# A windowed-attention and gated feed-forward kernel: sign words on GpSimd, one shift-and-sign instruction, and one eviction in two halves

## The chip, the cores and the metric

The kernel runs on one core of a Trainium2 chip. The metric is device time in microseconds (us) of one launch, as the median over several runs; lower is better. The core's engines are TensorE (PE in the profile, with PEld for its weight loads), VectorE (DVE), ScalarE (ACT), GpSimd (POOL) and SyncE (SP, which here only issues DMAs). Every engine works through its own queue in order, and engines wait for one another through semaphores.

## The reference

Eight heads of attention over 576 positions, batch 8, head dimension 64; heads 0 to 3 see the last 32 positions, heads 4 to 7 see every fourth of the last 128. Then a feed-forward layer on the 4608 tokens with 512 inputs and 2048 hidden units:

```python
scores = (q @ k.T) / 8, outside the mask -1e9
attn   = softmax(scores)
x      = (attn @ v) laid out as [4608, 512]
h      = x @ w_in                       # [512, 2048]
g      = h * clip(h + 3, 0, 6) / 6
out    = g @ w_out                      # [2048, 512], float32
```

`w_in` and `w_out` arrive as 64-bit floats. The kernel gets them as 64-bit words, and has to turn them into 32-bit floats itself.

## The kernel before

**Attention.** The 64 pairs of batch and head are worked in 48 "trios" of three 128-row parts (384 columns); each is a block of small 64-row matmuls for scores (L245), a largest value and an exponent, a transpose through TensorE (L374), a block of small matmuls for values (L255), a normalisation (L330 to L333), another transpose, and a split of the result into a high and a low part (L473, L479). The first twelve trios stand in the first stage.

**Weights.** There are 32 weight pieces of 128 by 512 elements: piece 2f is slab f of `w_in`, piece 2f+1 slab f of `w_out`. A piece p is loaded (`w`, L510) into a tile `st` of 64-bit words, that is, of a high and a low 32-bit word in turn, and then passes through these named steps:

- `Q` (`cv_round`, ACT, L529): the top bits of the low words, into `a`.
- `U` (`cv_product`, ACT, L525): the high words, read as 32-bit floats, times 2 to the power -112, into `v`.
- `s` (`cv_shift`, DVE, L533): `v` shifted left by three, in place.
- `j` (`cv_sign`, DVE, L539): the sign bit of the high words put into `v`, in place.
- `a` (`cv_add`, DVE, L546): `v` plus `a`, as integers.
- `h` (`cv_high`, ACT, L549) and `l` (`cv_low`, DVE, L555): the high part and the rest, which are what TensorE multiplies with.

**Feed-forward.** `G` (L571 to L573, twelve matmuls into one of two `ps_h` banks), `RE` (ACT, L579), `T` (DVE, L582, reads the bank and so frees it), `GH` (ACT or GpSimd, L586), `GL` (DVE, L590) and `H` (L632, nine matmuls). High and low parts make three products out of each one. The first `G` and `H` run while weights are still being turned; the later token groups run another scheme of seven products each (L784, L793 to L795), whose operands are sums of the weights.

**Order.** The first stage (to about 160 us) follows an order written out by hand, the string `ORDER` (L58 to L80): its names are issued in this order on ACT, DVE, SP and TensorE. `s4 CX4 j4` is step `s` of piece 4, a copy, and step `j` of piece 4. A name `w2@a0` is a load that SP holds back until `a0` is done; among the loads held back in this way are `k5@R3` (`R` is the largest value of a trio, L282), `v3@j0` and `v6@j2`. `Dn` stands for 2n fill matmuls on TensorE (L186). After the first stage a planner (`_in_time`) orders all engines from estimated durations. GpSimd has no order by hand in the first stage; its instructions are placed there by the framework's own scheduler, and there were none between the start and the planner's part.

**End.** In the last token group the last product (`T4`) is computed for its last two weight pairs one output half after the other (`parts` (0,) and then (1,)), each half one PSUM bank of 128 by 512. `scaled` (L1143) copies a bank to SBUF times one sixth on ACT (L1150), and `ship` (L1186) writes it out (L1190).

Of the kernel before, what the change touches and what calls it, by code (L numbers as in the profile page):

```python
# [13 lines left out]
U32 = mybir.dt.uint32  # L14
I64 = mybir.dt.int64
AF = mybir.ActivationFunctionType
ALU = mybir.AluOpType
# [7 lines left out]
CG = 512  # L25
# [61 lines left out]
def windowed_attention_ffn(ctx: ExitStack, tc: tile.TileContext, qk, vp, w, mask, out, out_t):  # L87
# [23 lines left out]
    nc = tc.nc  # L111
# [49 lines left out]
    def mask_of(kind, part, rows=P):  # L161
# [6 lines left out]
        out=ident, in_=ident, compare_op=ALU.not_equal, fill=1.0, base=0, pattern=[[-1, P]], channel_multiplier=1  # L168
# [32 lines left out]
    def w_tile(name, shape, dtype=F32):  # L201
        return wpool.tile([P, *shape], dtype, name=name, tag="w")
# [314 lines left out]
    def parts(p):  # L517
        st, va = staged[p]
        words = st.rearrange("p a n -> p (a n)").rearrange("p (n w) -> p n w", w=2)
        return words[:, :, 1], words[:, :, 0], va[:, 0], va[:, 1]  # L520
# [7 lines left out]
        _, lo_w, _, a = parts(p)  # L528
        return nc.scalar.mul(a.bitcast(U32), lo_w.bitcast(U32), 2.0**-29)  # L529

    def cv_shift(p):
        v = parts(p)[2]
        return nc.vector.tensor_scalar(  # L533
            out=v.bitcast(U32), in0=v.bitcast(U32), scalar1=3, scalar2=None, op0=ALU.logical_shift_left
        )

    def cv_sign(p):
        hi_w, _, v, _ = parts(p)
        return nc.vector.scalar_tensor_tensor(  # L539
            out=v.bitcast(U32), in0=hi_w.bitcast(U32), scalar=0x80000000, in1=v.bitcast(U32),  # L540
            op0=ALU.bitwise_and, op1=ALU.bitwise_or,
        )

    def cv_add(p):
# [256 lines left out]
    def load_mask(i):  # L801
# [13 lines left out]
        "Y": turn_x, "CX": turned_x,  # L815
        "XH": high, "XL": lambda t: low(t, nc.vector),

        "U": cv_product, "Q": cv_round, "s": cv_shift, "j": cv_sign, "a": cv_add, "h": cv_high, "l": cv_low,

        "G": gemm1, "RE": relu, "T": gate, "GH": gate_high, "GL": gate_low, "H": gemm2,  # L820
    }
# [3 lines left out]
    def op(engine, us, do, after=(), lag=0.0, takes=(), gives=(), before=(), ahead=AHEAD):  # L825
        plan.append(Operation(engine, us, do, [x for x in after if x is not None], lag, [(*x, 0)[:3] for x in takes], list(gives), list(before), ahead))
        if engine == "PE":
            beats.append(len(plan) - 1)
        return len(plan) - 1
# [309 lines left out]
    def second_products(g):  # L1139

        banks, lows, sums_of, os, made, read_by = {}, {}, {}, {}, {}, {}

        def scaled(name, bank, x, frees=False, parts=range(2)):  # L1143

            ops = []
            for d in parts:
                def do(d=d):
                    if name not in os:
                        os[name] = w_tile("o", [2, CG])
                    nc.scalar.mul(os[name][:, d], banks[bank][d], 1.0 / 6.0)  # L1150

                y = op("ACT", 0.6, do, [x], takes=() if d else SLOT, gives=FREE if frees else ())
                if frees:
                    freed.append(y)
                ops.append(y)
            made[name] = ops
            return ops
# [98 lines left out]
        def ends(p, x, parts):  # L1256

            if p == R11:
                read_by["x"] = read_by["y"] = seed(x)
            elif p == R21:  # L1260
                ship("11", scaled("11", "y", x, True))
            elif p == T1:
                read_by["w"] = scaled("22", "w", x)
            elif p == T2:
                read_by["x"] = scaled("12", "x", x)
            elif p == R22:
                ship("12", added("12", "w", x, True))
            elif p == T3:
                read_by["x"] = added("22", "x", x)
                ship("22", read_by["x"])  # L1270
            else:
                last_parts.extend(scaled("21", "x", x, True, parts))
                if len(parts) == 1:
                    ship("21", last_parts, slice(parts[0], parts[0] + 1))
                elif parts[-1] == 1:
                    ship("21", last_parts)
# [26 lines left out]
    with tc.manual_schedule(  # L1303
# [3 lines left out]
        for name in ORDER.split():  # L1307
            name, _, behind = name.partition("@")
# [261 lines left out]
```

## Time and profile before

| what | value |
|---|---|
| median of 3 runs | 825.68 us (823.89 to 826.71) |
| the profiled execution, its own time | 829.52 us |
| its span, first to last instruction | 827.7 us |
| TensorE busy | 814.9 us, 98% of the span |
| VectorE busy | 639.5 us, 77% |
| ScalarE busy | 512.4 us, 62% |
| GpSimd busy | 122.5 us, 15% |
| mean granted TensorE clock | 0.995 |

The page divides the span into 40 slices of 20.7 us. A row of a group gives the line, engine, operation, what it writes and reads, the shape and the count, then the busy time and the mean duration of one in ns, and the idle time of that engine before it with what ended it. A row of a timeline gives start and duration in us, engine, line and operation. A row of windows gives for each stretch its length and the busy time of every engine.

### The profile page before, as it was taken

What the parts mean: (1) busy time and instruction counts of PE and PEld (TensorE: products, weight loads), DVE (VectorE), ACT (ScalarE), POOL (GpSimd) and SP (SyncE); (2) the same over time, 40 slices, a digit from 0 to 9 for tenths busy, and PEclk for the clock granted to TensorE, in tenths of its full rate; (3) what the DMA queues carried; (4) which work ended last, traced back from release to release, by engine and by line L of the source; (5) the groups of instructions that cost most, each with busy time, mean ns of one, the idle gap of its engine ahead of it and who ended that gap; (6) DMA issues with size and microseconds to landing.
All of it is one profiled execution on the core that took longest, in us unless ns stands there. A gap on an engine that the chain in (4) does not pass through costs nothing.

```text
span 827.7 us, 20447 instructions
## 1 busy us (share of the span) xinstructions
PE 814.9 (98%) x8095; PEld 687.5 (83%) x8095; DVE 639.5 (77%) x1189; ACT 512.4 (62%) x1148; POOL 122.5 (15%) x268
## 2 busy tenths in 40 slices
PE   8799999999999999999999999999999999999998
PEld 5589989899888889878888888888888888888886
DVE  4699999568787998998989996575798934459943
ACT  3488776346877875677877565585565524446542
POOL 0000000013554454112360001031000000000000
PEclk9899999999999999999999999999999999999999
DMA  7847433336767879999985656786539369560632
GB/s 238 279 158 228 149 127 103 117 131 198 255 197 233 287 256 349 363 314 391 394 321 178 229 178 225 277 293 232 178 103 314 124 232 389 211 225 30 216 140 77
DMA packets 99343, 184.92 MB, mean 223 GB/s; under 512 B 6448, under 2 KB 35120, under 8 KB 99248
## 3 DMA queue, kind: packets, MB, share of 16 engines
q1 hardware_dynamic: 99248, 183.62, 64.4%
q8 instruction: 64, 1.05, 0.5%
q14 instruction: 31, 0.25, 0.1%
HBM read 144.79 MB, written 38.80 MB: 222 GB/s over the span
## 4 chain that ended last, share of the span: by engine, by line
PE 96%; ACT 2%; DVE 1%; issue 1%
PE ps_o L784 28%; PE ps_o L632 15%; PE ps_x L793 9%; PE ps_x L794 9%; PE ps_x L795 9%; PE ps_h L571 5%; PE ps_h L572 5%; PE ps_h L573 5%; PE ps_a L263 2%; PE ps_a L245 2%; PE ps_a L255 1%; PE ps_b L263 1%; PE ps_b L245 1%; PE ps_a L374 1%; PE idle L186 1%
## 5 line engine op out<-in xcount | busy, mean ns | idle before, releaser
L784 PE MATMUL ps_o<-gh,ring 128*128 128x512 f32 x672 | 182.5, 390 | 0.0
L784 PEld LDWEIGHTS ps_o<-gh,ring 128*128 128x128 f32 x672 | 126.2, 188 | 26.1
L1230 DVE TENSOR_TENSOR gl<-g,gh 128x512 fp32r<-128x512 f32 x168 | 109.1, 688 | 23.6 <-ACT gh L1226 17.8
L1226 ACT CAST gh<-g 128x512 fp32r<-128x512 f32 x168 | 97.0, 622 | 37.7 <-PE ps_o L784 36.8
L784 PE MATMUL ps_o<-gl,ring 128*128 128x512 f32 x336 | 103.8, 390 | 0.0
L632 PE MATMUL ps_o<-wo,gh 128*128 128x512 f32 x372 | 95.5, 392 | 0.0
L793 PE MATMUL ps_x<-cells,ring 128*128 128x512 f32 x240 | 94.1, 392 | 0.0
L795 PE MATMUL ps_x<-cells,ring 128*128 128x512 f32 x240 | 93.5, 390 | 0.0
L571 PE MATMUL ps_h<-x,wi 128*128 128x384 f32 x256 | 87.6, 342 | 0.0
L572 PE MATMUL ps_h<-x,wi 128*128 128x384 f32 x256 | 86.2, 337 | 0.0
L573 PE MATMUL ps_h<-x,wi 128*128 128x384 f32 x256 | 86.2, 337 | 0.0
L632 PEld LDWEIGHTS ps_o<-wo,gh 128*128 128x128 f32 x372 | 68.7, 188 | 11.5 <-DVE o L926 0.5
L784 PEld LDWEIGHTS ps_o<-gl,ring 128*128 128x128 f32 x336 | 63.1, 188 | 13.0
L794 PE MATMUL ps_x<-cells,ring 128*128 128x512 f32 x176 | 68.6, 390 | 0.0
L579 ACT ACTIVATE t<-ps_h,three 128x384 f32<-128x384 f32 x64 | 37.0, 581 | 41.0 <-PE ps_h L573 37.2
L794 PE MATMUL ps_x<-cell,ring 128*128 128x512 f32 x160 | 62.4, 390 | 0.0
L1198 DVE TENSOR_TENSOR g<-g 128x1024 f32<-128x1024 f32 x48 | 58.0, 1222 | 0.1
L586 POOL CAST gh<-t 128x384 fp32r<-128x384 f32 x36 | 24.4, 679 | 214.8 <-DVE t L582 200.0
L1095 DVE TENSOR_TENSOR g<-ps_x,g 128x512 f32<-128x512 f32 x48 | 33.1, 689 | 28.8 <-ACT g L1088 25.9
L1088 ACT COPY g<-ps_x 128x512 f32<-128x512 f32 x48 | 28.1, 586 | 42.6 <-PE ps_x L795 40.4
L793 PEld LDWEIGHTS ps_x<-cells,ring 128*128 128x128 f32 x240 | 45.1, 188 | 9.3
L795 PEld LDWEIGHTS ps_x<-cells,ring 128*128 128x128 f32 x240 | 45.1, 188 | 9.4
(137 smaller groups left out, 1665.3 us busy)
## 6 DMA issues: line engine op xcount, KB each, us to landing
ring<-sums SPq DMA_DIRECT2D x84, 512.0 KB, 8.6
ring<-rights SPq DMA_DIRECT2D x84, 512.0 KB, 4.8
st<-in_w SPq DMA_DIRECT2D x32, 512.0 KB, 4.4
kq<-in_qk SPq DMA_DIRECT2D x39, 416.0 KB, 4.6
v<-in_v SPq DMA_DIRECT2D x39, 390.0 KB, 5.8
sums<-wi SPq DMA_DIRECT2D x24, 256.0 KB, 6.8
rights<-wo SPq DMA_DIRECT2D x24, 256.0 KB, 6.1
out<-o SPq DMA_DIRECT2D x11, 512.0 KB, 3.3
```

The costliest lines, as they stand in the source:

```text
L571: nc.tensor.matmul(ph, lhsT=wt(f, 0)[:, ks], rhs=a, start=(kt == 0), stop=False)
L572: nc.tensor.matmul(ph, lhsT=wt(f, 0)[:, ks], rhs=b, start=False, stop=False)
L573: ins = nc.tensor.matmul(ph, lhsT=wt(f, 1)[:, ks], rhs=a, start=False, stop=(kt == NK - 1))
L579: return nc.scalar.activation(ts[n], phs[n], AF.Relu, bias=three, scale=1.0)
L632: ins = nc.tensor.matmul(po[c][tt], lhsT=g[:, tt * P : (tt + 1) * P], rhs=wt(f, row), start=(f == 0 and not i), stop=(f == NF - 1 and i == 2))
L784: nc.tensor.matmul(banks[part], lhsT=right[:, a, cols], rhs=x, start=(start and not i), stop=(i == 2), skip_group_check=True)
L793: nc.tensor.matmul(bank, lhsT=tile_[:, 0, ks], rhs=h[:, kt], start=(start and kt == 0), stop=False, skip_group_check=True)
L794: nc.tensor.matmul(bank, lhsT=tile_[:, 0, ks], rhs=l[:, kt], start=False, stop=False, skip_group_check=True)
L795: nc.tensor.matmul(bank, lhsT=tile_[:, 1, ks], rhs=h[:, kt], start=False, stop=(kt == 1), skip_group_check=True)
L1198: nc.vector.tensor_tensor(out=at[0], in0=at[1], in1=at[2], op=alu)
L1226: nc.scalar.copy(two[0], gated_tile(g, q, k))
L1230: nc.vector.tensor_tensor(out=two[1], in0=gated_tile(g, q, k), in1=two[0].bitcast(F32), op=ALU.subtract)
```

## The change

`s` becomes an instruction of GpSimd: it reads the high words as floats and writes, in their place in `st`, 2 to the power 31 as an integer where the float is negative, and 0 elsewhere. `j` becomes one VectorE instruction that shifts `v` left by three and puts the sign word in. The names keep their places in `ORDER`, and `a`, `h` and `l` are untouched. The last eviction of the kernel becomes two instructions of 128 by 256, the left half on ACT and the right half on DVE, with the same output DMA behind both.

```diff
+    def cv_sign(p):
+        hi_w = parts(p)[0]
+        return nc.gpsimd.tensor_scalar(
+            out=hi_w.bitcast(U32), in0=hi_w, scalar1=0.0, scalar2=2.0**31, op0=ALU.is_lt, op1=ALU.mult
+        )
+
     def cv_shift(p):
-        v = parts(p)[2]
-        return nc.vector.tensor_scalar(
-            out=v.bitcast(U32), in0=v.bitcast(U32), scalar1=3, scalar2=None, op0=ALU.logical_shift_left
-        )
-
-    def cv_sign(p):
-        hi_w, _, v, _ = parts(p)
+        sign, _, v, _ = parts(p)
         return nc.vector.scalar_tensor_tensor(
-            out=v.bitcast(U32), in0=hi_w.bitcast(U32), scalar=0x80000000, in1=v.bitcast(U32),
-            op0=ALU.bitwise_and, op1=ALU.bitwise_or,
+            out=v.bitcast(U32), in0=v.bitcast(U32), scalar=3, in1=sign.bitcast(U32),
+            op0=ALU.logical_shift_left, op1=ALU.bitwise_or,
         )
...
-        "U": cv_product, "Q": cv_round, "s": cv_shift, "j": cv_sign, "a": cv_add, "h": cv_high, "l": cv_low,
+        "U": cv_product, "Q": cv_round, "s": cv_sign, "j": cv_shift, "a": cv_add, "h": cv_high, "l": cv_low,
...
+                if parts == (1,):
+                    left, right = slice(0, CG // 2), slice(CG // 2, CG)
+                    ops.append(op("ACT", 0.35, lambda: nc.scalar.mul(os[name][:, 1, left], banks[bank][1][:, left], 1.0 / 6.0), [x]))
+                    ops.append(op("DVE", 0.35, lambda: nc.vector.tensor_scalar_mul(os[name][:, 1, right], banks[bank][1][:, right], 1.0 / 6.0), [x]))
+                    continue
                 y = op("ACT", 0.6, do, [x], takes=() if d else SLOT, gives=FREE if frees else ())
```

## The prediction

> **What bounds the kernel now.** I read the page's busy times first (the table above has them), then the windows, then TensorE's waits. A row of windows has the stretch, its length, the busy time (and count) of PE, PEld, DVE, ACT and POOL, the granted clock, the DMA share and GB/s.
>
> ```profile
> 0.00:60.00 60.00, 51.53 (x1254) 37.00 (x1254) 39.81 (x97) 34.69 (x78) 1.02 (x8) 0.94 0.69 233
> 60.00:160.00 100.00, 100.00 (x559) 91.25 (x558) 88.36 (x172) 70.84 (x134) 0.00 (x0) 1.00 0.46 150
> 160.00:820.00 660.00, 659.38 (x6271) 556.32 (x6270) 511.32 (x922) 405.71 (x934) 121.44 (x260) 1.00 0.68 236
> 820.00:827.70 7.70, 3.94 (x18) 2.94 (x16) 0.00 (x0) 1.20 (x2) 0.00 (x0) 0.92 0.18 68
> ```
>
> TensorE is idle for 12.9 us: 60 - 51.53 = 8.5 us in the first 60 us, nothing from 60 to 160 us, 0.6 us until 820 us, and 7.70 - 3.94 = 3.8 us at the end. A change that takes no matmul away can gain only in the first 60 us and in the tail. Between them it can only lose. The waits of the first part:
>
> ```profile
> PE ps_a L245 <- issue: 2.4, 1, 2.4
> PE ps_a L255 <- issue: 1.8, 3, 1.0
> PE ps_a L255 <- ACT e L309: 0.9, 1, 0.9
> ```
>
> The 4.2 us of "issue" waited for no engine. What a faster VectorE may shorten is the 0.9 us (whether an exponent ended it comes below) and a wait of 0.54 us shown there.
>
> **The work removed.** From the groups of VectorE, first from 16 to 159 us and then from 60 to 140 us:
>
> ```profile
> L533 DVE TENSOR_SCALAR va<-va 128x512 uint32<-128x512 uint32 x32 | 13.3, 422 | 5.5 <-ACT va L525 5.4
> ```
> ```profile
> 60.00:140.00 80.00, 80.00 (x459) 73.27 (x458) 75.65 (x149) 61.00 (x116) 0.00 (x0) 1.00 0.47 150
> ```
> ```profile
> L539 DVE SCALAR_TENSOR_TENSOR va<-st,va 128x512 uint32<-128x512 uint32 x24 | 16.3, 687 | 0.0
> L546 DVE CUSTOM_DVE_ANT_0 va<-va 128x1024 uint16<-128x1024 uint16 x24 | 16.1, 687 | 0.0
> L590 DVE TENSOR_TENSOR gl<-t,gh 128x384 fp32r<-128x384 f32 x20 | 11.1, 553 | 0.0
> L533 DVE TENSOR_SCALAR va<-va 128x512 uint32<-128x512 uint32 x24 | 9.9, 422 | 0.8 <-ACT va L525 0.8
> ```
>
> VectorE loses 32 shifts of 0.422 us, 13.5 us. The instruction that stays has the old `j`'s shape, operand steps and two bit operations, so I give it the same 687 ns. From 60 to 140 us this frees 24 x 0.42 = 10.1 us, but the matmuls cover all of it (80.00 of 80.00 busy): worth nothing there. Without that cover it would be worth at most those 10.1 us.
>
> **The price of a sign instruction.** The trace has no such GpSimd operation. Its nearest rows, all of GpSimd:
>
> ```profile
> L481 POOL COPY raw<-xf 128x160 f32<-128x160 f32 x7 | 3.3, 478 | 0.0
> L481 POOL COPY raw<-xf 128x224 f32<-128x224 f32 x2 | 1.2, 591 | 0.0
> L479 POOL TENSOR_TENSOR x<-xf,x 128x384 fp32r<-128x384 f32 x2 | 2.0, 1013 | 1.6 <-ACT x L473 1.6
> L586 POOL CAST gh<-t x36: 496/508/1437, 168.8 to 340.6; 128x384 fp32r<-128x384 f32 x36
> ```
>
> Lower end: the cast's fastest 496 ns, dense, scaled from 384 to 512 elements, 0.66 us. Upper end: the two-input instruction scaled likewise, 1.35 us. Between: the copies that write every fourth word cost (591 - 478)/64 = 1.77 ns per element, so 0.591 + 288 x 0.00177 = 1.10 us at 512. The sign reads and writes every second word, between the dense and the every-fourth case: I take 0.9 us, and 0.1 us for each of the semaphores before and behind it. So `j` can start 1.1 us after `U` ends. GpSimd runs nothing from 60 to 160 us, so 32 x 0.9 = 29 us fit and no queue of its own is passed.
>
> **The first 24 us, where VectorE stands on the path.** Timelines of VectorE, ACT, SP and TensorE:
>
> ```profile
> 16.21 0.43 DVE L533 TENSOR_SCALAR va<-va 128x512 uint32<-128x512 uint32 x1 [1.00 <-ACT va L525]
> 16.56 0.16 DVE L330 TENSOR_SCALAR z<-ps_a 128x6 f32<-128x6 f32 x1
> ...
> 17.91 0.68 DVE L539 SCALAR_TENSOR_TENSOR va<-st,va 128x512 uint32<-128x512 uint32 x1
> ```
> ```profile
> 15.52 0.66 ACT L525 ACTIVATE va<-st 128x512 f32<-128x512 f32 x1
> ```
> ```profile
> 18.62 0.33 SPq L222 DMA_DIRECT2D first<-in_v  x1
> ```
> ```profile
> 20.70 0.52 PE L374 MATMUL ps_a<-ident,x 128*128 128x128 f32 x3 [0.54 <-DVE x L333]
> ...
> 23.36 0.21 PE L255 MATMUL ps_a<-first,a 64*32 64x65 f32 x1 [0.90 <-ACT e L309]
> ```
>
> Piece 0's shift makes VectorE wait 1.00 us for `U0`, with a normalisation (L330) queued behind it. With the shift gone, that normalisation can start at 16.21 - 1.00 = 15.2 instead of 16.56 us. `j0` then waits for GpSimd: `U0` ends at 16.18, so `j0` starts at 17.3 instead of 17.91, 0.6 us earlier. Behind it stand the next trio's difference, `a0` and the normalisation for which TensorE waits at 20.70 us, and the load `v3` that SP holds until `j0` is done (18.62). The page blames the wait at 23.36 us on an exponent that this block doesn't read. The block does read `v3`, and a load of that line takes this long to land:
>
> ```profile
> DMA to landing us min/median/max: 4.0/5.2/7.9
> ```
>
> 18.62 + 4.0 is 22.6 us at the earliest, so I take `v3` as the releaser. The two waits lie in one chain, so they don't add: the gain is the 0.6 us by which `j0` moves, at most the 0.90 us of the second wait, and zero if earlier loads fill the DMA queue. I take 0.5 us.
>
> **Where the new wait costs.** `j` now waits for two engines in turn. That hurts where the shift stood directly behind `U`; the first such place is piece 6:
>
> ```profile
> 44.14 0.68 ACT L525 ACTIVATE va<-st 128x512 f32<-128x512 f32 x1
> ```
> ```profile
> 45.32 0.69 DVE L539 SCALAR_TENSOR_TENSOR va<-st,va 128x512 uint32<-128x512 uint32 x1
> ...
> 47.70 0.55 DVE L582 SCALAR_TENSOR_TENSOR t<-t,ps_h 128x384 f32<-128x384 f32 x1
> ```
> ```profile
> 48.77 0.42 PE L571 MATMUL ps_h<-x,wi 128*128 128x384 f32 x1
> ```
>
> `j6` moves from 45.32 to 44.82 + 1.1 = 45.9 us, and with it the queue behind it up to the gate (L582), which frees the bank for the third `G`. The gate ends at 48.25 + 0.6 = 48.85, and `G` starts at 48.77: 0.15 us of TensorE's time. With a sign of 0.66 us it costs nothing, with one of 1.35 us that also waits out one 0.69 us VectorE instruction 1.3 us. Piece 26, late in the stage, has room:
>
> ```profile
> 154.80 0.69 DVE L555 TENSOR_TENSOR wi<-va,wi 128x512 fp32r<-128x512 f32 x1
> ```
> ```profile
> 156.78 0.19 PEld L571 LDWEIGHTS ps_h<-x,wi 128*128 128x128 f32 x1
> ```
>
> Its low part ends at 155.49, and would at 156.1; the `G` that reads it starts at 156.78.
>
> **The tail.** The last copy, with rows of smaller copies on both engines:
>
> ```profile
> 823.98 0.60 ACT L1150 ACTIVATE o<-ps_o 128x512 f32<-128x512 f32 x1 [0.76 <-PE ps_o L784]
> ```
> ```profile
> L306 ACT ACTIVATE e<-e,mx 128x64 f32<-128x64 f32 x24 | 6.3, 368 | 2.1 <-DVE mx L298 2.1
> ```
> ```profile
> L330 DVE TENSOR_SCALAR z<-ps_a 128x6 f32<-128x6 f32 x12 | 1.9, 162 | 8.7 <-PE ps_a L255 8.6
> L926 DVE TENSOR_SCALAR o<-ps_o 128x512 f32<-128x512 f32 x2 | 1.4, 688 | 0.3 <-PE ps_o L632 0.3
> ```
>
> Interpolated to 256 columns: ACT 0.368 + 0.232 x 192/448 = 0.47 us, VectorE 0.162 + 0.526 x 250/506 = 0.42 us. VectorE is idle there, so the DMA is issued 0.60 - 0.47 = 0.13 us earlier. Bounds: 0.3 us if time went purely by columns, and 0.1 us lost if SP's second wait costs more than is gained.
>
> **The sum.** -0.5 + 0.15 - 0.13 = -0.5 us, so 829.0 us against the profiled execution's own 829.52 us. That execution is 3.8 us above the median, so the forecast keeps the difference: 825.68 - 0.5 = 825.2 us. Its own range, by the bounds above, runs from -1.2 (0.9 and 0.3) to +1.4 (1.3 and 0.1): 824.5 to 827.1 us.
>
> **Rival 1, slower: GpSimd's reads hold VectorE up.** From 60 to 140 us the kinds with two SBUF inputs (L539, L546 and L590 above, and these) are busy 16.3 + 16.1 + 11.1 + 8.9 + 6.9 = 59.3 of 75.65 us, 78%.
>
> ```profile
> L555 DVE TENSOR_TENSOR wo<-va,wo 128x512 fp32r<-128x512 f32 x13 | 8.9, 687 | 1.3 <-ACT wo L549 1.2
> L555 DVE TENSOR_TENSOR wi<-va,wi 128x512 fp32r<-128x512 f32 x10 | 6.9, 688 | 0.0
> ```
>
> If each sign shut such an instruction out for its whole time, VectorE would lose 0.78 x 0.9 = 0.70 us per sign and save 0.42. Over 24 signs that is 6.7 us more work against 80 - 75.65 = 4.35 us of idle time, so TensorE waits 2.4 us: 827.6 us. With a 1.1 us sign it is 0.86 - 0.42 = 0.44 us each, 10.5 us, and 831.4 us; I put the rival at the middle, 829.5 us. It decides from a loss of 0.60 us per sign on (0.42 + 4.35/24). Against it, the same VectorE instruction without and with GpSimd at work (50 to 160 and 199 to 420 us):
>
> ```profile
> L590 DVE TENSOR_TENSOR gl<-t,gh x27: 543/552/560, 50.0 to 155.4; 128x384 fp32r<-128x384 f32 x27
> ```
> ```profile
> L590 DVE TENSOR_TENSOR gl<-t,gh x30: 516/552/694, 200.6 to 343.0; 128x384 fp32r<-128x384 f32 x30
> ```
>
> The median stays at 552 ns and the longest grows by 0.13 us, while GpSimd's cast grows from 496 to as much as 1437 ns: mostly GpSimd waits. Chance 12%.
>
> [...]
>
> **Rival 2: the half clock goes away.**
>
> ```profile
> 34.50:41.33 6.83, 6.01 (x112) 3.65 (x112) 2.31 (x8) 0.00 (x0) 0.00 (x0) 0.50 0.65 226
> ```
>
> For 6.83 us TensorE ran at half clock, right after its 2.4 us wait. At full clock the 6.01 us would take about 3.0: 825.2 - 3.0 = 822.2 us. For it: TensorE arrives at that wait up to 0.5 us earlier, among other transfers. Against it: the wait itself is an "issue" one, which nothing in the change touches. Chance 14%.
>
> **Rival 3: the change does nothing.** The DMA queue, not `v3`'s issue, sets the second wait; signs are hidden; only the tail's 0.13 us remain: 825.5 us. For it: the DMA share of 0.69 in the first 60 us. Against it: the 1.00 us stall at 16.21 us does go. Chance 16%.
>
> **How the numbers follow.** Forecast 58%, rivals 12, 14 and 16%. The predicted time is the forecast's 825.2 us. The range reaches to rival 2 and to the lower part of rival 1: 822.0 to 828.4 us. A measurement of this kernel can tell about 0.3% (2.5 us) from no change. Faster by more than that is rival 2 and a little else, 16%; slower is most of rival 1, 9%; within it 75%.
>
> **What would show it.** GpSimd should have 32 instructions of some 0.9 us before 160 us; VectorE should lose some 13 us of busy time in its first 160 us, with `j`, `a` and `l` still near 687 ns; TensorE's wait of 0.90 us should shrink and its busy share from 60 to 160 us stay whole; the last copy should show two rows of 0.4 to 0.5 us. Signs above 2 us, idle TensorE after 60 us, or a half clock at another place or none would prove me wrong.

## The result, and the profile after

The changed kernel takes 832.57 us (median of 10 runs, 830.84 to 839.02); the kernel before, run beside it on the same chip, takes 825.69 us (median of 10, 823.89 to 827.89). The ratio on record is 1.0095, with a 95% interval from 1.0071 to 1.012. (The ratios in this document are the ones on record, which differ a little from the quotients of the medians.) By the medians the change costs 6.9 us, by the ratio 7.8 us. The prediction said 825.2 us, no change that can be measured, with a range up to 828.4 us. It was wrong.

The profiled execution of the changed kernel has an own time of 832.06 us and a span of 830.2 us. Its span is only 2.5 us longer than the one before (827.7 us), because the profiled execution before was itself 3.8 us above its median, and the half clock from 34.50 to 41.33 us, for which the prediction reckons about 3.0 us, is not in this one. So the place of the loss is looked for in the stages, not in the difference of the two spans.

Three rows of windows of the kernel after, with the columns as in the prediction (length, busy time and count of PE, PEld, DVE, ACT and POOL, granted clock, DMA share, GB/s), and the stretch of the old half clock:

```profile
0.00:60.00 60.00, 51.80 (x1275) 38.45 (x1276) 41.73 (x102) 36.89 (x84) 15.10 (x15) 1.00 0.71 235
60.00:160.00 100.00, 96.07 (x523) 84.41 (x521) 80.37 (x132) 66.71 (x127) 52.21 (x25) 1.00 0.45 148
160.00:820.00 660.00, 659.65 (x6274) 556.64 (x6274) 513.42 (x926) 406.87 (x936) 121.45 (x260) 1.00 0.68 236
34.50:41.33 6.83, 6.73 (x129) 5.90 (x128) 4.75 (x12) 4.36 (x10) 1.27 (x1) 1.00 0.90 313
```

From 60 to 160 us TensorE was busy for 100.00 of 100 us; now it is for 96.07, so it stands idle for 3.9 us. In the same stretch it issues 523 matmuls where it issued 559, which at 100/559 = 0.18 us each would be 6.4 us of work; matmul records can be missing, so this count is rough. The gates on VectorE (L582), one for each `G`, tell the place better. Against the kernel with the faster sign, shown further down, which has the same VectorE instructions, the tenth gate starts at 80.15 us (80.21 us there), the fifteenth at 103.91 (101.49), the twenty-third at 142.30 (135.90) and the twenty-eighth at 163.02 (156.51). So some 6 us are lost between 80 and 142 us, and after that nothing more. VectorE's busy time in this stage *fell*, from 88.36 to 80.37 us: it has less to do than before and still comes too late.

What it does instead of working is in the waits of VectorE, 16 to 160 us (engine, line, waited for; total us, times, longest), and in those of TensorE, 60 to 160 us:

```profile
DVE va L539 <- POOL st L533: 20.7, 17, 4.7
```
```profile
PE ps_h L571 <- DVE t L582: 2.7, 4, 1.5
```

And the sign instruction itself, among GpSimd's groups up to 170 us; below it, the two VectorE groups next to it, 16 to 165 us:

```profile
L533 POOL TENSOR_SCALAR st<-st 128x512 uint32<-128x512 f32 x32 | 66.3, 2085 | 90.1 <-ACT va L525 78.1 <-DVE gl L590 11.3 <-DVE va L539 0.8
```
```profile
L539 DVE SCALAR_TENSOR_TENSOR va<-va,st 128x512 uint32<-128x512 uint32 x32 | 25.3, 795 | 20.7 <-POOL st L533 20.7
L546 DVE CUSTOM_DVE_ANT_0 va<-va 128x1024 uint16<-128x1024 uint16 x32 | 23.3, 742 | 0.1
```

A sign takes 2.085 us, not 0.9. VectorE stands still for it in 17 of the 32 pieces, 20.7 us in all, and 4.7 us in the worst one. One place shows how that reaches TensorE. GpSimd, VectorE and TensorE of the kernel after, 133 to 143 us (start, duration, engine, line, operation, count, and in brackets the idle time before it with its releaser):

```profile
133.35 6.62 POOL L533 TENSOR_SCALAR st<-st 128x512 uint32<-128x512 f32 x3 [4.20 <-DVE gl L590]
```
```profile
135.79 1.13 DVE L539 SCALAR_TENSOR_TENSOR va<-va,st 128x512 uint32<-128x512 uint32 x1 [0.88 <-POOL st L533]
136.84 0.68 DVE L555 TENSOR_TENSOR wo<-va,wo 128x512 fp32r<-128x512 f32 x1
...
138.04 1.14 DVE L539 SCALAR_TENSOR_TENSOR va<-va,st 128x512 uint32<-128x512 uint32 x1
...
140.01 0.69 DVE L539 SCALAR_TENSOR_TENSOR va<-va,st 128x512 uint32<-128x512 uint32 x1 [0.23 <-POOL st L533]
...
142.30 0.55 DVE L582 SCALAR_TENSOR_TENSOR t<-t,ps_h 128x384 f32<-128x384 f32 x1
```
```profile
142.90 0.44 PE L571 MATMUL ps_h<-x,wi 128*128 128x384 f32 x1 [1.48 <-DVE t L582]
```

Three signs stand in a row, 6.62 us, and set the pace: the three `j` start at 135.79, 138.04 and 140.01 us, one for each sign. Behind them in VectorE's queue stands a gate (L582), which reads nothing of the weights. It starts at 142.30 us, ends at 142.85, and frees the bank for which TensorE has by then waited 1.48 us.

The rows also show a second effect: two of the three `j`, those that run while a sign runs, take 1.13 and 1.14 us, the third 0.69 us. But not all instructions beside a sign grow: the low part at 136.84 us, which also has two inputs in SBUF, runs while the signs run and keeps its 0.68 us.

### The profile page after: what moved, and what is told of

The parts are those of the page before. It is cut to its first block, busy times and chain, and to the rows that moved or that the text cites. A ratio compares the mean times of both kernels' runs of the same rounds, so it can differ in the third digit from the quotient of the medians.

```text
span 830.2 us, 20475 instructions
## 1 busy us (share of the span) xinstructions
PE 813.8 (98%) x8095; PEld 684.4 (82%) x8095; DVE 635.9 (77%) x1158; ACT 511.4 (62%) x1148; POOL 188.8 (23%) x300
## 4 chain that ended last, share of the span: by engine, by line
PE 87%; DVE 4%; POOL 3%; DMA 2%; issue 2%; ACT 1%; POOLq 0%
PE ps_o L784 28%; PE ps_o L632 12%; PE ps_x L793 9%; PE ps_x L795 9%; PE ps_x L794 9%; PE ps_h L571 4%; PE ps_h L573 4%; PE ps_h L572 4%; POOL st L533 3%; PE ps_a L263 2%; DMA st<-in_w 1%; PE ps_a L245 1%; PE ps_b L263 1%; PE ps_b L245 1%; DVE va L539 1%
## 5 line engine op out<-in xcount | busy, mean ns | idle before, releaser
L533 POOL TENSOR_SCALAR st<-st 128x512 uint32<-128x512 f32 x32 | 66.3, 2085 | 90.1 <-ACT va L525 78.1
L412 POOL COPY a<-a_t 32x192 f32<-32x192 f32 x72 | 31.2, 433 | 142.8 <-DVE a L405 121.8
L571 PEld LDWEIGHTS ps_h<-x,wi 128*128 128x128 f32 x256 | 48.1, 188 | 8.9 <-DVE t L582 4.6
L793 PEld LDWEIGHTS ps_x<-cells,ring 128*128 128x128 f32 x240 | 45.1, 188 | 9.3
```

The source lines that it names most:

```text
L533: return nc.gpsimd.tensor_scalar(out=hi_w.bitcast(U32), in0=hi_w, scalar1=0.0, scalar2=2.0**31, op0=ALU.is_lt, op1=ALU.mult)
L571: nc.tensor.matmul(ph, lhsT=wt(f, 0)[:, ks], rhs=a, start=(kt == 0), stop=False)
L793: nc.tensor.matmul(bank, lhsT=tile_[:, 0, ks], rhs=h[:, kt], start=(start and kt == 0), stop=False, skip_group_check=True)
```

## The experiments

Each ratio is against the runs of the kernel before beside it on the same chip, with the 95% interval.

**The parts one at a time.** The first question was which part loses. The tail alone, put into the kernel before:

```diff
+                if parts == (1,):
+                    ops.append(op("ACT", 0.35, ... left half ...))
+                    ops.append(op("DVE", 0.35, ... right half ...))
+                    continue
```

> The kernel before with the split of the last eviction alone. The theory of the wait (the changed kernel is slower because each sign takes 2.0 us on GpSimd and VectorE stands in its queue until it is done) expects no loss here: ratio 0.999 to 1.001, the last copy two rows of about 0.4 us in place of one of 0.60 us, 0.1 to 0.2 us gained. The rival that the tail costs something (SyncE waiting for two engines) expects 1.001 or more.

Measured 826.34 us, 1.0008 (0.9992 to 1.0024): it doesn't move the time. So the loss is in the signs. The rows of the end of this kernel, VectorE and ScalarE:

```profile
820.22 0.42 DVE L1155 TENSOR_SCALAR o<-ps_o 128x256 f32<-128x256 f32 x1 [7.42 <-PE ps_o L784]
820.68 0.38 ACT L1154 ACTIVATE o<-ps_o 128x256 f32<-128x256 f32 x1 [1.22 <-DVE o L1155]
```

The two halves don't run beside each other: ScalarE starts when VectorE is done. They take 820.68 + 0.38 - 820.22 = 0.84 us, the one copy before took 0.60.

The reads of GpSimd without a wait: in the kernel before, the new sign instruction is issued in place behind `j`, and nobody waits for its result.

```diff
-        return nc.vector.scalar_tensor_tensor(
+        ins = nc.vector.scalar_tensor_tensor(
...
+        nc.gpsimd.tensor_scalar(
+            out=hi_w.bitcast(U32), in0=hi_w, scalar1=0.0, scalar2=2.0**31, op0=ALU.is_lt, op1=ALU.mult
+        )
+        return ins
```

> The kernel before, with VectorE's shift and sign as they were, and the new GpSimd instruction issued in addition, in place on the high words once VectorE has read them; no engine waits for its result except a later load into the same tile. The theory of the wait expects most of the loss to be gone: ratio 1.000 to 1.003, GpSimd's 32 instructions still 2.0 us each, VectorE's wait for GpSimd 0. The theory of contention (GpSimd's reads lengthen VectorE's instructions with two SBUF inputs, by about 0.43 us each time the two overlap) expects a loss of the changed kernel's kind, 1.005 or more, with the means of the VectorE lines for the sign, the add and the low part at 740 to 800 ns instead of 687.

Measured 830.06 us, 1.0056 (1.0039 to 1.0073). The window from 60 to 160 us, and the group of `a`, the instruction behind `j`, which now runs beside a sign:

```profile
60.00:160.00 100.00, 98.04 (x532) 87.85 (x531) 92.99 (x160) 67.14 (x126) 57.83 (x27) 0.98 0.45 146
```
```profile
L550 DVE CUSTOM_DVE_ANT_0 va<-va 128x1024 uint16<-128x1024 uint16 x32 | 26.6, 845 | 0.1
```

`a` grows from 687 to 845 ns on the mean, and VectorE, which here keeps its shifts, is busy for 92.99 of 100 us. The loss is the one that the theory of contention expected: reads of GpSimd alone can cost time where VectorE is as full as that. In the kernel after it isn't: with the VectorE work of the kernel after and the same sign, again issued behind `j` so that nothing waits for it:

```diff
     def cv_sign(p):
-        hi_w = parts(p)[0]
-        return nc.gpsimd.tensor_scalar(...)
+        return issued[f"U{p}"]
 
     def cv_shift(p):
...
+        nc.gpsimd.tensor_scalar(
+            out=sign.bitcast(U32), in0=sign, scalar1=0.0, scalar2=2.0**31, op0=ALU.is_lt, op1=ALU.mult
+        )
+        return ins
```

> The changed kernel with the same VectorE work, and the same 2.0 us sign on GpSimd, but issued behind the instruction that should use it, so that VectorE waits for no sign (the signs of the weights are wrong: that part of the computation is left out). GpSimd still reads SBUF next to the add and the low part. The theory of the wait expects 0.997 to 1.001, since nothing stands still; the theory of contention expects 1.004 or more, with TensorE's busy time from 60 to 160 us at 98 of 100 us or less as in the run with the sign beside the old pair.

```profile
L540 POOL TENSOR_SCALAR st<-st 128x512 uint32<-128x512 f32 x32 | 69.6, 2188 | 83.0 <-DVE va L536 64.3 <-ACT a L387 10.6 <-ACT wo L550 3.0
```
```profile
L547 DVE CUSTOM_DVE_ANT_0 va<-va 128x1024 uint16<-128x1024 uint16 x32 | 26.5, 841 | 0.1
```

Measured 826.1 us, 1.002 (1.0005 to 1.0035). The signs take 2.19 us here, and the adds are as long as in the run before (841 ns), but without the wait only some 0.2% of the 0.95% is left: a little more than the theory of the wait expected (1.001 at most), and half of what the theory of contention did.

**What the wait costs by itself.** Signs replaced by GpSimd instructions that only write: memsets of the sign words, as many as are needed to fill the sign's time. `j` waits for them as it does for a sign.

```diff
-        return nc.gpsimd.tensor_scalar(... is_lt, mult)
+        for n in (512, 512, 512, 256):
+            ins = nc.gpsimd.memset(hi_w[:, :n], 0.0)
+        return ins
```

> The changed kernel with the sign replaced by four GpSimd memsets of the same words to zero (three of 512 words and one of 256, about 2.0 to 2.2 us together by the forms measured alone), so that VectorE waits as long as in the changed kernel, but GpSimd reads nothing from SBUF (all signs come out positive: that part of the computation is left out). The theory of the wait expects the loss to stay: 1.006 to 1.011, VectorE's wait for GpSimd 18 us or more, its add at 687 ns. The theory of contention expects it to go: 1.003 or less.

```profile
60.00:160.00 100.00, 95.66 (x523) 84.64 (x523) 73.56 (x132) 67.24 (x127) 48.27 (x100) 1.00 0.47 149
```
```profile
L534 POOL MEMSET st<- 128x512 f32 x96 | 52.8, 567 | 92.6 <-ACT va L525 79.6 <-DVE gl L590 10.7
L534 POOL MEMSET st<- 128x256 f32 x32 | 10.3, 333 | 1.1
```
```profile
L539 DVE SCALAR_TENSOR_TENSOR va<-va,st 128x512 uint32<-128x512 uint32 x31 | 21.2, 689 | 29.0 <-POOL st L534 29.0
L546 DVE CUSTOM_DVE_ANT_0 va<-va 128x1024 uint16<-128x1024 uint16 x31 | 20.8, 685 | 0.1
```

Measured 835.88 us, 1.0109 (1.0085 to 1.0134). Three memsets of 567 and one of 333 ns are 2.03 us of work (some 2.2 us from the first start to the last end in the timeline), about as much as a sign, and neither `j` nor `a` becomes longer (689 and 685 ns). A wait of about the sign's length is enough for the whole loss, without any reads, and TensorE issues the same 523 matmuls from 60 to 160 us as in the kernel after.

With three and with two memsets of 512 words, 3 x 567 = 1.70 and 2 x 567 = 1.13 us by the row above:

```diff
+        for _ in range(3):        # the other kernel: range(2)
+            ins = nc.gpsimd.memset(hi_w, 0.0)
+        return ins
```

> As the four memsets, but three of 512 words (about 1.7 us together, as long as the doubled float sign, whose ratio was 1.013): a wait of that length without any reading of SBUF by GpSimd (all signs positive: that part of the computation is left out). If the wait alone makes the doubled float sign's loss: 1.008 to 1.013. If GpSimd's reading adds to it: 1.002 to 1.007.

> Two memsets of 512 words (about 1.15 us together, as long as the sign of half the words, whose ratio was 0.9985; signs positive, that part left out): by the theory of the wait 0.997 to 1.001, since most of what VectorE has queued between U and the new instruction covers it.

```profile
L539 DVE SCALAR_TENSOR_TENSOR va<-va,st 128x512 uint32<-128x512 uint32 x31 | 21.2, 689 | 20.6 <-POOL st L534 20.6
```

Measured 829.25 us, 1.0043 (1.0025 to 1.0062) with three, and 825.11 us, 0.9997 (0.9983 to 1.0012) with two. The row is that of three. So the price of the wait is not in proportion to its length: nothing at 1.1 us, 0.4% at 1.7 us, 1.1% at 2.0 us. With three memsets VectorE stands as long as in the kernel after (20.6 and 20.7 us), and the kernel loses less than half as much. The rest of the loss after is likely to come from the instructions that the signs' reads lengthen; this run doesn't show that part by itself.

**A faster sign.** A float times 2 to the power -126 twice leaves a zero that keeps the sign: the same sign word without a comparison, complete in its result.

```diff
-            out=hi_w.bitcast(U32), in0=hi_w, scalar1=0.0, scalar2=2.0**31, op0=ALU.is_lt, op1=ALU.mult
+            out=hi_w, in0=hi_w, scalar1=2.0**-126, scalar2=2.0**-126, op0=ALU.mult, op1=ALU.mult
```

> The changed kernel with the sign word made in another way: the high word times 2 to the power -126, twice, which underflows to plus or minus zero, float in and float out, same tile, same steps, so no conversion to an integer and no comparison. If the comparison or the conversion makes the 2.0 us, the sign falls to 0.7 to 1.2 us, VectorE's wait for GpSimd from 20.7 us to under 8 us, and the ratio to 0.998 to 1.003. If the steps of two words or the mere two operations make it, the sign stays at 2.0 us and the ratio at 1.007 to 1.012.

> The float sign (product by 2 to the power -126, twice) once more, in five rounds: the same 0.998, with an interval that settles whether it beats the kernel before. By the theory of the wait it is 0.997 to 0.999, the first 45 us being shorter and no wait being left behind them; by the rival of nothing 0.999 to 1.001.

```profile
L533 POOL TENSOR_SCALAR st<-st 128x512 f32<-128x512 f32 x32 | 26.2, 818 | 122.3 <-ACT va L525 103.3 <-DVE gl L590 13.0 <-DVE wo L555 3.9
```
```profile
L539 DVE SCALAR_TENSOR_TENSOR va<-va,st 128x512 uint32<-128x512 uint32 x32 | 23.5, 741 | 6.0 <-POOL st L533 5.9
```
```profile
60.00:160.00 100.00, 100.00 (x554) 90.82 (x554) 83.95 (x141) 68.76 (x130) 21.19 (x25) 1.00 0.45 148
```

Measured 824.91 us, 0.9981 (0.9968 to 0.9994), and the second time 825.34 us, 0.9995 (0.9981 to 1.0009). With a sign of 818 ns TensorE is whole again from 60 to 160 us, and everything but the sign's form is as in the kernel after. The first interval lies just below 1, the second doesn't: the kernel is no better than before by anything that two measurements agree on.

A sign that is shorter in another way, the comparison for the first 256 of the 512 words:

```diff
-            out=hi_w.bitcast(U32), in0=hi_w, ...
+            out=hi_w[:, :256].bitcast(U32), in0=hi_w[:, :256], ...
```

> The changed kernel with the sign made for the first 256 of the 512 words of each piece only (the other half of the weights gets wrong signs and exponents, so this part of the computation is left out). The theory of the wait expects the sign at 1.0 to 1.1 us, VectorE's wait for GpSimd to fall from 20.7 us to under 8 us, and a ratio of 0.998 to 1.003. The theory of contention expects half of the overlap and so about half of the loss to stay, 1.004 to 1.006.

```profile
L533 POOL TENSOR_SCALAR st<-st 128x256 uint32<-128x256 f32 x32 | 38.3, 1206 | 108.2 <-ACT va L525 90.4 <-DVE gl L590 12.2 <-DVE wo L555 3.9
```

Measured 824.64 us, 0.9985 (0.9968 to 1.0002). The sign is a little longer than expected, and VectorE's wait for it falls to 9.4 us, not under 8. A sign of 1.21 us is free all the same, like two memsets. It is the time that counts, not the comparison.

**The same work twice.** The fast sign issued twice, some 1.65 us for `j` to wait for:

```diff
+        for _ in range(2):
+            ins = nc.gpsimd.tensor_scalar(
+                out=hi_w, in0=hi_w, scalar1=2.0**-126, scalar2=2.0**-126, op0=ALU.mult, op1=ALU.mult
+            )
+        return ins
```

> The float sign with its GpSimd instruction issued twice in a row (the second leaves plus or minus zero as it is), so a sign is ready about 1.6 to 1.7 us after U, between the 0.82 us of the float sign and the 2.09 us of the changed kernel; the output is complete. By the theory of the wait the loss sets in once the sign outlasts what VectorE has queued between U and the new instruction (0.5 to 5 us, mostly 1 to 2): 1.001 to 1.006. If instead the comparison itself did something harmful apart from its duration, 0.998 to 1.001.

```profile
L541 DVE SCALAR_TENSOR_TENSOR va<-va,st 128x512 uint32<-128x512 uint32 x31 | 23.3, 758 | 15.4 <-POOL st L534 14.6 <-ACT x L473 0.8
```

Measured 835.1 us, 1.0131 (1.0113 to 1.0149). That is a miss: it loses more than the kernel after, with a shorter wait (14.6 against 20.7 us). What was missing showed in the same pair without a wait, issued behind `j` as above:

```diff
+        for _ in range(2):
+            nc.gpsimd.tensor_scalar(out=sign, in0=sign, scalar1=2.0**-126, scalar2=2.0**-126, op0=ALU.mult, op1=ALU.mult)
+        return ins
```

> The doubled float sign's two GpSimd instructions issued behind the instruction that should use them, so that nothing waits, while GpSimd reads SBUF at its fastest for 1.65 us per piece (signs wrong: that part left out). If GpSimd's reading adds much to the doubled float sign's loss: 1.004 or more. If the wait alone makes it: 0.998 to 1.002.

```profile
L548 DVE CUSTOM_DVE_ANT_0 va<-va 128x1024 uint16<-128x1024 uint16 x32 | 30.6, 967 | 0.1
L536 DVE SCALAR_TENSOR_TENSOR va<-va,st 128x512 uint32<-128x512 uint32 x32 | 24.4, 766 | 3.7 <-ACT va L525 3.7
```

Measured 830.59 us, 1.0069 (1.0046 to 1.0092). Here VectorE's add takes 967 ns beside two fast signs, where it took 841 beside one slow sign. The reads alone cost 0.7%, and 1.7 us of waiting alone 0.4% (three memsets); together 1.1%, and the doubled sign lost 1.3%, which the intervals allow. That the two simply add up isn't shown. So two things count, the time for which `j` waits and the reads that GpSimd does in it, and two fast signs read the words twice where the slow one reads them once.

**The sign's forms by themselves.** Eleven forms of GpSimd instruction, three times each on one tile ahead of everything else, before the first load:

```diff
+    for _ in range(3):
+        nc.gpsimd.tensor_scalar(out=odd.bitcast(U32), in0=odd, scalar1=0.0, scalar2=2.0**31, op0=ALU.is_lt, op1=ALU.mult)
+        nc.gpsimd.tensor_scalar(out=odd, in0=odd, scalar1=0.0, scalar2=2.0**31, op0=ALU.is_lt, op1=ALU.mult)
+        nc.gpsimd.tensor_scalar(out=dense.bitcast(U32), in0=dense, scalar1=0.0, scalar2=2.0**31, op0=ALU.is_lt, op1=ALU.mult)
...
+        nc.gpsimd.tensor_scalar(out=odd, in0=odd, scalar1=2.0**-126, scalar2=2.0**-126, op0=ALU.mult, op1=ALU.mult)
+        nc.gpsimd.tensor_scalar(out=odd, in0=odd, scalar1=2.0**-126, scalar2=None, op0=ALU.mult)
+        nc.gpsimd.tensor_copy(out=odd, in_=odd)
+        nc.gpsimd.tensor_scalar(out=odd, in0=odd, scalar1=0.0, scalar2=None, op0=ALU.is_lt)
...
```

> The kernel before, with GpSimd instructions put ahead of everything (the first load is held until they are done, so that no other engine works meanwhile): each of eleven forms three times on one tile of 128 by 1024 floats. If the conversion to an integer costs, then the sign's form takes 2.0 us and the same comparison and product with a float output about 0.8 us, both for every second word and dense. If the comparison costs, both take about 2.0 us and the product by 2 to the power -126, twice, about 0.8 us. If the step of two words costs, the dense forms are faster than the stepped ones by more than 0.3 us.

The groups of GpSimd by line, in this order (`odd` is every second word; L234 is the sign of the kernel after, L235 the same with a float output, L236 the sign on dense words, L238 two products, L239 one product, L240 a copy, L241 one comparison):

```profile
L234 POOL TENSOR_SCALAR bench<-bench 128x512 uint32<-128x512 f32 x3 | 5.9, 1973 | 0.2
L235 POOL TENSOR_SCALAR bench<-bench 128x512 f32<-128x512 f32 x3 | 5.9, 1964 | 0.2
L236 POOL TENSOR_SCALAR bench<-bench 128x512 uint32<-128x512 f32 x3 | 5.8, 1920 | 0.2
...
L238 POOL TENSOR_SCALAR bench<-bench 128x512 f32<-128x512 f32 x3 | 1.9, 639 | 0.2
L239 POOL TENSOR_SCALAR bench<-bench 128x512 f32<-128x512 f32 x3 | 4.6, 1542 | 0.2
L240 POOL COPY bench<-bench 128x512 f32<-128x512 f32 x3 | 1.9, 632 | 0.2
L241 POOL TENSOR_SCALAR bench<-bench 128x512 f32<-128x512 f32 x3 | 4.6, 1532 | 0.3
```

The sign costs 1.97 us with no other engine at work, so nearly all of its 2.09 us in the kernel is its own price and not that of contention. Neither the stride (1973 against 1920 ns dense) nor the conversion to integers (1973 against 1964) makes it dear. Two products take 639 ns, as long as a copy (632); one product alone takes 1542 ns, and so does one comparison (1532). Why the form with two products is that fast and the others aren't, these rows can't tell.

**The sign somewhere else.** The fast sign written over the low words, so that it needs `Q` and not `U` to be done:

```diff
-            out=hi_w, in0=hi_w, scalar1=2.0**-126, scalar2=2.0**-126, op0=ALU.mult, op1=ALU.mult
+            out=lo_w, in0=hi_w, scalar1=2.0**-126, scalar2=2.0**-126, op0=ALU.mult, op1=ALU.mult
...
-        sign, _, v, _ = parts(p)
+        _, sign, v, _ = parts(p)
```

> The float sign (product by 2 to the power -126, twice) written over the low words instead of the high ones: it then needs the low words read (Q), and no longer has to come after U, which is mostly the later of the two. By the theory of the wait VectorE's wait for GpSimd falls from the float sign's 5.9 us to 3 us or less, and the ratio is at or a little under the float sign's 0.998: 0.996 to 0.999. By the rival nothing is left to gain: TensorE is already without a wait from 60 to 160 us, so the same 0.998.

```profile
0.00:60.00 60.00, 52.55 (x1260) 37.83 (x1261) 39.87 (x96) 35.97 (x82) 6.33 (x16) 0.94 0.71 233
60.00:160.00 100.00, 100.00 (x558) 91.26 (x557) 83.78 (x142) 70.46 (x132) 21.51 (x24) 1.00 0.47 150
```
```profile
L539 DVE SCALAR_TENSOR_TENSOR va<-va,st 128x512 uint32<-128x512 uint32 x32 | 23.3, 732 | 4.9 <-POOL st L533 4.9
```

Measured 828.39 us, 1.0044 (1.0029 to 1.0059): a miss. The wait fell from 5.9 to 4.9 us only, and the kernel is slower. TensorE is whole from 60 to 160 us; in the first 60 us its granted clock is 0.94, as it was in the profiled execution of the kernel before. In the profile it is a half clock again (0.50 from 34 to 37 us), and its gates stand 1.4 to 2.8 us later than with the fast sign, from the first one on. Only one of the four runs was profiled; the mean clock of the four is 0.995, 0.995, 0.995 and 0.998, where the nine runs of the kernel before beside them have 0.997 to 1.000. So this kernel seems to meet the half clock more often; why it does is left open, and whether that is the whole loss too.

**The head.** The prediction's gain there came from a VectorE that no longer waits for `U0` with a normalisation behind it. The same can be had in the kernel before, by moving `s0` in `ORDER` behind what it held up:

```diff
-E2 k6@E2 s0 Z1 CA2 D1 B4 R3 k5@R3 j0
+E2 k6@E2 Z1 CA2 D1 B4 R3 k5@R3 s0 j0
```

> The kernel before with one entry of the order moved: piece 0's shift behind the normalisation, the largest value and its load, directly ahead of piece 0's sign (in the string, s0 goes from before Z1 to before j0). GpSimd has no part in it. It tests the forecast's step of the first 24 us by itself: VectorE no longer stands for 1.00 us in front of the normalisation. Expected by that step: the sign of piece 0 starts 0.4 to 0.8 us earlier, TensorE's two waits near 20.7 and 23.4 us shrink, and the ratio is 0.998 to 1.000. By the rival (the DMA queue paces these loads) 0.9995 to 1.0005 and the wait near 23.4 us stays.

> The kernel before, unchanged, timed against itself: both theories expect 0.998 to 1.002. Its profile is wanted without the half clock from 34.5 to 41.3 us that the profiled execution had; if that half clock comes and goes by itself, this execution or the spread of its times shows it.

The first fence shows the kernel with `s0` moved, VectorE and TensorE; the second, the kernel before profiled once more, TensorE alone:

```profile
17.01 0.69 DVE L539 SCALAR_TENSOR_TENSOR va<-st,va 128x512 uint32<-128x512 uint32 x1
...
23.46 0.32 PE L355 MATMUL ps_a<-mi 32*128 32x384 bf16 x1 [1.57 <-issue]
```
```profile
23.38 0.21 PE L255 MATMUL ps_a<-first,a 64*32 64x65 f32 x1 [0.95 <-DMA first<-in_v]
```

Measured 825.49 us, 1.0002 (0.9989 to 1.0014), and 826.62 us, 1.0009 (0.9993 to 1.0025), for the kernel before against itself. `j0` starts at 17.01 us, and TensorE's wait for the load of `v3` is gone. In its place stands a wait of 1.57 us, put down to "issue", at the same time. Nothing is gained.

## Why the prediction was wrong

**The step that failed: the price of a sign instruction.** The term was 0.9 us, between 0.66 and 1.35 us; it measured 2.085 us in the kernel and 1.97 us alone. The rows from which it was scaled were copies and casts and a two-input instruction. I took the sign for a copy with another stride. A copy does cost what the lower end said (632 ns for 512 elements, every second word), but the stride, for which the price went up from 0.66 to 0.9 us, makes 0.05 us (1973 against 1920 ns): what the sign costs beyond a copy comes with its operations, not its operands. No row of the trace before had a GpSimd instruction with such operations, so the upper end had no right to be called an end. The prediction did name signs above 2 us and an idle TensorE after 60 us as what would prove it wrong, and both came.

With a sign inside the bounds the total comes out: at 0.82 us the time is 824.9 and 825.3 us, at 1.21 us 824.6 us, where the forecast said 825.2. That is no proof of its terms. They add up to half a microsecond, which these runs can't tell from nothing, and two of the three are not borne out below. What the fast sign shows is rival 3, a change that does nothing.

**Where the new wait costs: right in its mechanism, and mis-sized by the same price.** The prediction named piece 6 and the way from `j` over the queue to the gate and its bank. Timelines of GpSimd, VectorE and TensorE after:

```profile
40.06 2.01 POOL L533 TENSOR_SCALAR st<-st 128x512 uint32<-128x512 f32 x1 [9.29 <-ACT va L525]
```
```profile
42.10 0.69 DVE L539 SCALAR_TENSOR_TENSOR va<-va,st 128x512 uint32<-128x512 uint32 x1 [2.03 <-POOL st L533]
...
44.38 0.55 DVE L582 SCALAR_TENSOR_TENSOR t<-t,ps_h 128x384 f32<-128x384 f32 x1
```
```profile
44.98 0.44 PE L571 MATMUL ps_h<-x,wi 128*128 128x384 f32 x1 [0.81 <-DVE t L582]
```

`j6` starts 0.03 us after the sign ends (40.06 + 2.01 = 42.07), where 0.1 us was taken for the semaphore. TensorE waits 0.81 us for the gate, where 0.15 us was forecast and no wait stood before. What the prediction left out is that pieces follow one another: it judged the late pieces by piece 26 alone, and said that GpSimd would pass no queue of its own because all signs together fit into its idle time. At 2.09 us three signs in a row hold up three `j` (the 6.62 us above), and such places lie between 60 and 160 us, where "it can only lose" was said and nothing charged.

**The work removed: right, and worth nothing, as said.** The new `j` takes the old one's time, as said, where no read is beside it (689 ns beside memsets). One can draw up a balance of VectorE's time. It saves 32 x 0.422 = 13.5 us of shifts, and the 5.4 us for which they waited for `U`. Against that stand 20.7 us of waiting and longer instructions, 32 x (0.795 - 0.687 + 0.742 - 0.687) = 5.2 us: 7.0 us more than what was saved, about the size of the loss. The same balance gives 29.0 - 18.9 = 10.1 us for the four memsets, measured 9.0 us (1.09% of 825 us), and 20.6 - 18.9 = 1.7 us for three, measured 3.5 us (0.43%). For two fast signs without a wait it doesn't hold: 3.7 us of waiting and 32 x (0.967 - 0.687 + 0.766 - 0.687) = 11.5 us stand against 18.9, so VectorE should be 3.7 us better off, and the kernel loses 0.69%, 5.7 us. There the low parts (838 and 740 ns instead of 687) and `gl` (637 instead of 553 ns) grow too, by 5.6 us in all; with them the balance is a loss of 1.9 us, still too little. For the doubled sign with its wait it is 14.6 + 6.1 - 18.9 = 1.8 us by `j` and `a` (758 and 808 ns), 8.2 us with the low parts (827 and 747 ns) and `gl` (683 ns), and measured 1.31%, 10.8 us. So the balance is a rough account that fits the slow sign and the memsets, and falls short beside fast signs; what is missing there, these runs don't settle.

**Rival 1, the reads: real, and not what decides.** Beside a sign, `j` takes 1.13 us instead of 0.69. By themselves, with the same sign and no wait, the reads cost 0.2% of the 0.95%; together with the wait they count for more, since three memsets with the same 20.6 us of standing lose 0.43%. A wait of the sign's length without reads loses it all (four memsets), reads of the sign without the wait a fifth. The prediction gave this rival 0.70 us per sign and a point of 0.60 us from which it decides; by the longer `j` and `a` above it is 0.16 us per sign, and 0.21 us with the low parts and `gl` (711 and 576 ns), so these alone stay below that point.

By the Trainium skill, "SBUF — State Buffer", section "Who interferes with whom", a VectorE instruction with two SBUF inputs contends with a GpSimd instruction that reads SBUF and not with one that only writes it. The trace agrees on which: 742 ns for the add beside signs that read, 685 ns beside memsets. A VectorE instruction shut out for a sign's whole time, as the prediction had it, the runs don't show. In the timelines of the kernel after, up to 160 us, the sixteen instructions with two SBUF inputs that take over 0.06 us more than usual all begin within about half a microsecond of a sign's start; nineteen others lie wholly later within a sign and keep their length, like the low part at 136.84 us above. As far as these runs go, it is the number of signs that lengthens VectorE's work, and hardly their length: in all, by the means of `j`, `a`, the low parts and `gl`, each sign adds 0.17 us (fast sign), 0.21 us (kernel after), 0.25 us (slow sign, no wait) or 0.27 us (two fast ones, no wait).

**Rival 2, the half clock: it happened, by itself.** It is gone in the profiled execution after (clock 1.00 from 34.50 to 41.33 us) and gone too when the kernel before was profiled again:

```profile
0.00:60.00 60.00, 51.31 (x1266) 37.44 (x1266) 42.35 (x104) 36.11 (x82) 1.02 (x8) 1.00 0.69 233
```

It comes and goes between executions of one kernel. The prediction's way of keeping the 3.8 us between the profiled execution and the median was right: ten runs of the kernel before have their median at 825.69 us.

**The first 24 us: half right, and worth nothing.** The load `v3` is what TensorE waited for at 23.36 us, as said against the page: profiled again, the kernel before shows that load as the releaser. But `j0` doesn't come forward. Everything in this execution stands up to 1 us earlier than in the one before, so the time is taken from `U0`. ScalarE, VectorE and TensorE after, and VectorE and ScalarE with the fast sign:

```profile
14.82 0.65 ACT L525 ACTIVATE va<-st 128x512 f32<-128x512 f32 x1
```
```profile
17.60 0.69 DVE L539 SCALAR_TENSOR_TENSOR va<-va,st 128x512 uint32<-128x512 uint32 x1 [1.97 <-POOL st L533]
```
```profile
20.40 0.52 PE L374 MATMUL ps_a<-ident,x 128*128 128x128 f32 x3 [1.43 <-DVE x L333]
22.34 0.21 PE L255 MATMUL ps_a<-first,a 64*32 64x65 f32 x1 [0.18 <-ACT x L473]
```
```profile
15.31 0.66 ACT L525 ACTIVATE va<-st 128x512 f32<-128x512 f32 x1
```
```profile
16.75 0.69 DVE L539 SCALAR_TENSOR_TENSOR va<-va,st 128x512 uint32<-128x512 uint32 x1 [0.30 <-POOL st L533]
```

From the start of `U0` to that of `j0` it was 17.91 - 15.52 = 2.39 us before; it is 2.78 us after and 1.44 us with the fast sign. So with about the price that the prediction gave the sign its 0.6 us do come, even 0.95. With the real price `j0` is 0.4 us late, and TensorE's first wait grows to 1.43 us where it was 0.54, while the second falls from 0.90 to 0.18 us; a later load of the same kind then holds TensorE up for 1.42 us at 28.33 us. And an earlier `j0` brought no gain in the one run that has it alone: with `s0` moved in the kernel before, `j0` came 0.9 us earlier (`U0` starts at 15.52 us there too), an "issue" wait took the place of the other, and the time stayed.

**The tail: wrong in its sign, too small to measure.** The prediction let both halves run at once. The widths were right (0.42 us on VectorE as said, 0.38 on ScalarE instead of 0.47). In the kernel after, as in the rows of the tail alone above, ScalarE starts behind VectorE, at 826.78 us where VectorE started at 826.32. 826.78 + 0.38 - 826.32 = 0.84 us, so 0.24 us are lost instead of 0.13 gained. The profile names VectorE's half as what ended ScalarE's wait. The two halves lie in one PSUM bank. The Trainium skill, "PSUM — Partial Sum Buffer", section "PSUM bank collisions raise a hardware error", states that two engines must not be on the same bank and partitions at the same time, reads included and even at other columns, and that semaphores have to keep them apart. The rows agree with it, and the step should have gone by it; that the bank is the reason for the order here is argued, since no run has the halves in two banks.

## What to carry to other kernels

Price an instruction from a row of the same operation on the same engine; where the trace has none, another operation of the same shape is no upper bound, and the answer is to ask from which price on the forecast turns over (here between 1.2 and 1.7 us) and to give that case a chance. Work moved to an idle engine is free only while its latency fits in front of the one who waits: on an engine that works in order, everything behind the wait is late with it, even if that engine has less to do than before. And before an eviction is split over two engines, ask whether its halves lie in one bank: here the two halves of one bank ran one behind the other, and took longer than the whole.

## What was not expected of the hardware

- GpSimd's `tensor_scalar` on 128 x 512 floats takes 639 ns with two products, 1542 with one product, 1532 with one comparison and 1964 with a comparison and a product.
- What GpSimd's reads cost VectorE goes by the number of its instructions rather than by their length: VectorE's add took 967 ns beside two signs of 0.90 us, and 841 ns beside one of 2.19 us. Memsets don't lengthen it at all (685 ns).
- In this kernel the price of a wait set in steeply: memsets of 1.13 us per piece cost nothing, 1.70 us 0.4%, 2.03 us 1.1%.
